# Attention and mixer kernel: row-wise weight loads, strided weight columns, one load on another queue, features one stage earlier

## The chip, the cores and the metric

The kernel runs on one core of one Trainium2 chip. The metric is the device time of one execution in microseconds (us). The five engines are TensorE (PE; its weight loads are listed apart as PEld), VectorE (DVE), ScalarE (ACT), GpSimd (POOL) and SyncE (SP). ACT, POOL and SP also have queues from which DMAs are issued (written ACTq, POOLq, SPq).

## The reference

Linear attention with cosine and sine features, whose output is the input of a token mixer and a channel mixer. There are 8 batches of 8 heads, 576 positions and a head size of 64, all in float32.

```python
q_p = phi(q, cos_w, sin_w)          # relu(x) * cos, relu(x) * sin, side by side: 128 features
k_p = phi(k, cos_w, sin_w)
kv = np.einsum('bhsf,bhsd->bhfd', k_p, v)
z = np.sum(k_p, axis=2)
num = np.einsum('bhsf,bhfd->bhsd', q_p, kv)
den = np.einsum('bhsf,bhf->bhs', q_p, z)[..., None] + 1e-06
x = num / den                       # per batch 576 x 512
h = np.maximum(x.T @ w_tok1, 0.0) @ w_tok2      # 576 -> 256 -> 576, over positions
u = x + h.T
h2 = np.maximum(u @ w_ch1, 0.0) @ w_ch2         # 512 -> 1536 -> 512, over channels
out = u + h2
```

## The kernel before, in words

A batch's 576 positions are four chunks of 128 (row p of the tile holds positions 4p to 4p+3, one to each chunk) and a tail of 64. The tails of two batches share the 128 partitions of one tail tile, so a tail's channel mixer is done once for two batches, in the odd one. Chunks are numbered 0 to 3, the tail is R = 4.

A batch goes through two halves. *Front* (class Front): features of keys (k_side, KS) and queries (q_side, QS), each two DVE instructions (L263) that write kp or qp; values cast to bf16 (values, V: L274 on ACT, L276 elsewhere); kv_ps, the product of features and values (kv, L320); kv_out; the transposes of the query features, by DMA from SP (q_trans_dma, L350), in batches 0 and 1 on PE (q_trans, L340); numerators and division (num, L359 to L369, into x_sb); the token mixer (tok1, tok2: b_ps L382, u_ps L406, u_sb and u_tail L409); the cast of u to bf16 and its transposes by DMA (u_trans_dma L438, tail_trans_dma L443). *Channel* (class Channel): twelve steps c_main(mi), each four matmuls of 128 w_ch1 columns (the stationary operand) with uT into c_ps (L535), and ACT's relu into h1T (L539); in odd batches c_tail does the same for the tail pair with 128 moving columns (ct_ps, L555); then o_step, two matmuls of w_ch2 at a time into o_ps (L568), the addition o_sb on DVE (L573), and the output DMA from SP (L575). Batch 0's first three c_ps are done block by block (L545).

Order on every engine is the order of the program, written out by hand. While Channel of batch b is issued step by step, pieces of Front of batch b+1 are put between the steps. The method pieces lists them as (step, what, arguments): steps 0 to 11 (C + at) are the c steps, from O = 12 on the o steps. Batch 1 has a plan of its own (first), which also holds batch 0's last tok2; batch 2 takes its values some steps later than the others (late). Entries at step -1 are issued just ahead of the channel half. The main loop (L728 to L752) builds the plan at the start of each channel half.

Loads: q, k and v of a batch come as one DMA of 1 MB each and one or two of 128 KB for the tails, all from SP's queue after the start. load_batch(2, "v") stands at step NCH + 13 of batch 0, so on SP it follows the three transposes of batch 1's u (L438 twice, L443). The weights w_ch1 and w_ch2 come from POOL's queue with a cast from float32 to bf16: w_ch1 in four DMAs (two blocks of 128 rows and half the columns each, L184 to L191), w_ch2 in three (four blocks of 128 rows each, L194 to L198). The first w_ch1 load waits for the keys of batch 0, batch 1's loads wait for the second w_ch1 load, and batch 2's keys for the second w_ch2 load.

The hidden channels are in blocks of 128, mi or ki from 0 to 11: c_main writes block mi of h1T, o_step multiplies block ki of h1T by w_ch2[:, ki, :]. The tiles kp and qp have four buffers, PSUM has four of tag mm (c_ps, ct_ps, o_ps and others) and two of tag at.

Of the kernel before, what the change touches and what calls it, by code (L numbers as in the profile page):

```python
# [16 lines left out]
def kernel(  # L17
# [15 lines left out]
    nc = tc.nc  # L33
# [147 lines left out]
        nc.gpsimd.memset(t[half(1)], 0.0)  # L181
    for g in range(2):
        nc.gpsimd.dma_start(out=w_tail1[half(g), :], in_=moe_w_tok1[SM:S, :])
    C2 = D_ch // 2  # L184
    w_ch1_done = []
    for c2 in range(2):
        for ki in range(0, NCC, 2):
            w_ch1_done.append(nc.gpsimd.dma_start(
                out=w_ch1[:, ki:ki + 2, c2 * C2:(c2 + 1) * C2],
                in_=moe_w_ch1[ki * P:(ki + 2) * P, c2 * C2:(c2 + 1) * C2]  # L190
                .rearrange("(n c) d -> c n d", c=P)))  # L191
    after(w_ch1_done[0], k_done)
    w_ch2_done = []
    def load_w_ch2():  # L194
        for ki in range(0, NCH, 4):
            w_ch2_done.append(nc.gpsimd.dma_start(
                out=w_ch2[:, ki:ki + 4, :],
                in_=moe_w_ch2[ki * P:(ki + 4) * P, :].rearrange("(n t) d -> t n d", t=P)))  # L198

# [14 lines left out]
    class Front:  # L216
# [244 lines left out]
        def pieces(self, b, before):  # L461


            first, odd = b == 1, b % 2 == 1
            V, KV, N = self.values, self.kv, self.num
            KS, QS, QT, T = self.k_side, self.q_side, self.q_trans, self.tok2
            C, O = 0, NCH
            if first:

                u, act, pool = before.tok2, nc.scalar, nc.gpsimd  # L470
                plan = [(4, KS, 0), (4, KS, 1), (5, u, 0, ps_at, False), (5, KS, 2, True),
                        (6, KS, 3, True), (6, u, 1, ps_at, False), (7, KS, R), (8, V, 0, act),
                        (8, V, 2, pool), (8, V, 3, pool), (8, load_w_ch2),
                        (8, u, 2, None, False), (9, V, 1, act), (9, u, 3, None, False),
                        (10, u, R, None, False), (10, V, R, nc.vector)]
                plan += [(11, KV, ci) for ci in range(NSC)]
                plan += [(11, QS, 0), (11, QS, 1), (11, self.kv_out),
                         (11, QT, 0, (0, H), act, ps_at), (11, QT, 1), (11, QS, 2), (11, QS, R),
                         (O, QT, 2), (O, N, 0), (O, QS, 3), (O + 1, QT, R, (0, H), act, ps_at),
                         (O + 1, N, 1), (O + 3, N, 2), (O + 3, QT, 3),  # L480
                         (O + 5, N, R), (O + 7, N, 3), (O + 8, before.tail_cast)]
            else:

                late = b == 2
                plan = [(C + at, V, ci, nc.scalar)
                        for ci, at in enumerate((3, 3, 4, 4, 5) if late else (-1, -1, 0, 1, 2))]
                plan += [(C + at, KS, ci) for ci, at in enumerate((0, 0, 1, 2, 2))
                         if ci < R or not odd]
                for ci, at in zip(ORDER, (0, 0, 1, 0, 2) if odd else (1, 2, 3, 4, 5)):
                    if ci < R or not odd:  # L490
                        plan += [(C + at, QS, ci), (C + at, self.q_trans_dma, ci)]

                plan += [(C + at, KV, ci) for ci, at in
                         enumerate((4, 5, 5, 6, 7) if late else
                                   (2, 3, 4, 5, 6) if odd else (2, 3, 4, 6, 7))]
                plan.append((C + (6 if odd else 7), self.kv_out))
            if first:
                at, mix, t = (), O + 7, O + 11
            elif odd:
                at, mix, t = (C + 8, C + 9, C + 10, C + 11, O + 2), O + 3, O + 7  # L500
            else:
                at, mix, t = (C + 9, C + 10, C + 11, O + 1, O + 3), O + 4, O + 8
            plan += [(i, N, ci) for i, ci in zip(at, ORDER)]
            plan += [(mix, self.mix_head, 0), (mix + 1, self.mix_head, 1),
                     (mix + 2, self.mix_tail)]

            plan += [(t + at, T, ci) for ci, at in enumerate((0, 1, 2, 3, 3) if not first else
                                                             (0, 0, 1, 2, 2))]
            plan += [(t + 3 - first, self.u_trans_dma, 3, R)]
            plan.append((t + 2 - first, self.u_trans_dma, 0, 3))  # L510
            if odd:
                plan.append((t + 3 - first, self.tail_trans_dma))
            slots = {}
            for slot, what, *args in sorted(plan, key=lambda p: p[0]):
                slots.setdefault(slot, []).append((what, args))
            return slots
# [4 lines left out]
    class Channel:  # L521
# [7 lines left out]
        def c_main(self, mi, lo=0, hi=SM):  # L529
            if lo == 0:  # L530
                self.c_ps[mi] = ps_mm.tile([P, SM], F32, name="c_ps", tag="mm")
            c_ps = self.c_ps[mi]
            uT = self.res["uT"].rearrange("p (r k) t -> p r k t", r=R)
            for ki in range(NCC):
                nc.tensor.matmul(c_ps[:, lo:hi], w_ch1[:, ki, mi * P:(mi + 1) * P],  # L535
                                 uT[:, lo // P:hi // P, ki, :],
                                 start=(ki == 0), stop=(ki == NCC - 1))
            if hi == SM:
                nc.scalar.activation(self.h1T[:, mi, :], c_ps, AF.Relu)  # L539

        def c_block(self, mi, ki):
            if ki == 0:
                self.c_ps[mi] = ps_mm.tile([P, SM], F32, name="c_ps", tag="mm")
            uT = self.res["uT"].rearrange("p (r k) t -> p r k t", r=R)
            nc.tensor.matmul(self.c_ps[mi], w_ch1[:, ki, mi * P:(mi + 1) * P], uT[:, :, ki, :],  # L545
                             start=(ki == 0), stop=(ki == NCC - 1))
            if ki == NCC - 1:
                nc.scalar.activation(self.h1T[:, mi, :], self.c_ps[mi], AF.Relu)

        def c_tail(self, mi):  # L550

            if mi % R == 0:
                self.ct_ps = ps_mm.tile([P, R, P], F32, name="ct_ps", tag="mm")
            for ki in range(NCC):
                nc.tensor.matmul(self.ct_ps[:, mi % R, :], w_ch1[:, ki, mi * P:(mi + 1) * P],  # L555
                                 self.tail.uT[:, ki, :], start=(mi % R == 0 and ki == 0),
                                 stop=(mi % R == R - 1 and ki == NCC - 1), skip_group_check=True)
            if mi % R == R - 1:
                nc.scalar.activation(self.h1T_tail[:, mi - R + 1:mi + 1, :], self.ct_ps, AF.Relu)
# [140 lines left out]
                c.c_block(mi, kb)  # L700
        return c

    def load_batch(b, which="kvq", behind=None):
        if b not in io_tiles:
            io_tiles[b] = tiles()
        if b // 2 not in io_tails:
            io_tails[b // 2] = tail_tiles()
        qt, vt, kt = io_tiles[b]
        qtt, vtt, ktt = io_tails[b // 2]
        done = []  # L710
        for n in which:
            dst, tail_dst, src = {"k": (kt, ktt, k), "v": (vt, vtt, v), "q": (qt, qtt, q)}[n]
            done.append(load_main(dst, src, b))
            if behind is not None and len(done) == 1:
                after(done[0], behind)
            if b % 2 == 0:
                load_tail(tail_dst, src, b)
            if b % 2 == 0 or b == 1:
                load_tail(tail_dst, src, b | 1)
        return done  # L720


    results = [dict() for _ in range(B)]
    load_batch(1, "kvq", behind=w_ch1_done[1])
    tails = {0: tail0}
    f = Front(0, results[0], tail0)
    c = first_front(f)
    for b in range(B):  # L728
        slots = {}
        if b + 1 < B:  # L730
            if (b + 1) // 2 not in tails:
                tails[(b + 1) // 2] = Tail((b + 1) // 2)
            slots = Front(b + 1, results[b + 1], tails[(b + 1) // 2]).pieces(b + 1, f)
        if b > 0:
            c = Channel(b, results[b], tails[b // 2])
        for what, args in slots.pop(-1, ()):
            what(*args)
        for i, step in enumerate(c.steps(AHEAD if b == 0 else 0)):
            step()
            for what, args in slots.pop(i, ()):  # L740
                what(*args)
# [2 lines left out]
            if b == 0 and i == NCH:  # L744
                load_batch(2, "kq", behind=w_ch2_done[1])
            if b == 0 and i == NCH + 13:
                load_batch(2, "v")
            if 0 < b < B - 2 and i == NSC:
                load_batch(b + 2, "vq")
            if b < B - 3 and i == NCH + (18 if b == 0 else 12):  # L750
                load_batch(b + 3, "k")
        assert not slots  # L752

    _ = tile, bass_utils

# [29 lines left out]
```

## Time and profile before

| what | value |
|---|---|
| median of three runs | 273.86 us (273.8 to 275.31) |
| profiled execution, own time | 273.98 us |
| its span, first to last instruction | 271.8 us |
| granted TensorE clock | 0.997 |
| DVE busy | 165.0 us (61%) |
| ACT busy | 129.7 us (48%) |
| 512-column matmuls of L535 | x360 |
| 128-column matmuls of L555 | x192, 219 ns each |
| weight loads over w_ch1, L535 / L555 | x384 / x192, 97 and 98 ns each |
| w_ch loads, issue to landing | 5.8 / 9.9 / 12.1 us (min, median, max) |

The profile was taken of one execution; its own time lies above its span by what surrounds the first and last instruction. Matmuls are pipelined: a matmul's listed duration runs from its start to the end of its last column, and the next starts before that, so throughput is read from starts, and an idle time in brackets is shorter than what was lost by the starts.

### The profile page before, as it was taken

What the parts mean: (1) busy time and instruction counts of PE and PEld (TensorE: products, weight loads), DVE (VectorE), ACT (ScalarE), POOL (GpSimd) and SP (SyncE); (2) the same over time, 40 slices, a digit from 0 to 9 for tenths busy, and PEclk for the clock granted to TensorE, in tenths of its full rate; (3) what the DMA queues carried; (4) which work ended last, traced back from release to release, by engine and by line L of the source; (5) the groups of instructions that cost most, each with busy time, mean ns of one, the idle gap of its engine ahead of it and who ended that gap; (6) DMA issues with size and microseconds to landing.
All of it is one profiled execution on the core that took longest, in us unless ns stands there. A gap on an engine that the chain in (4) does not pass through costs nothing.

```text
span 271.8 us, 5106 instructions
## 1 busy us (share of the span) xinstructions
PE 260.4 (96%) x2030; PEld 138.6 (51%) x2050; DVE 165.0 (61%) x376; ACT 129.7 (48%) x228; POOL 10.9 (4%) x24
## 2 busy tenths in 40 slices
PE   6989999997999999999999999999999999999994
PEld 2665465454644445446644445446644445445543
DVE  5974888767366477659466567659465567720022
ACT  4955975427616273347606363437606362426400
POOL 6400220000000000000000000000000000000000
PEclk9999999999999999999999999999999999999998
DMA  7999999979994989759994879389974380180032
GB/s 219 344 270 284 326 152 247 309 180 351 189 337 116 268 155 253 229 138 251 160 362 115 277 188 316 111 164 267 217 266 116 116 147 10 41 211 3 2 102 91
DMA packets 91815, 53.68 MB, mean 197 GB/s; under 512 B 59408, under 2 KB 86928, under 8 KB 91792
## 3 DMA queue, kind: packets, MB, share of 16 engines
q1 hardware_dynamic: 88432, 49.62, 67.3%
q0 software_dynamic: 2832, 3.21, 7.2%
q10 hardware_dynamic: 528, 0.52, 0.6%
q8 instruction: 16, 0.26, 0.4%
q14 instruction: 7, 0.06, 0.1%
HBM read 35.85 MB, written 9.44 MB: 167 GB/s over the span
## 4 chain that ended last, share of the span: by engine, by line
PE 77%; DVE 15%; DMA 4%; issue 2%; SPq 1%; ACT 0%; DVEq 0%
PE o_ps L568 32%; PE c_ps L535 19%; PE u_ps L406 6%; PE b_ps L382 6%; DVE qp L263 5%; PE ct_ps L555 4%; DVE kp L263 4%; PE num_ps L359 3%; DVE x_sb L369 3%; PE kv_ps L320 2%; DMA vt<-in_v_dram 2%; DMA qt<-in_q_dram 2%; PE idle_ps L204 1%; PE c_ps L545 1%; DVE den L367 1%
## 5 line engine op out<-in xcount | busy, mean ns | idle before, releaser
L568 PE MATMUL o_ps<-w_ch,h1T 128*128 128x512 bf16 (+1 forms) x381 | 92.5, 372 | 0.5
L535 PE MATMUL c_ps<-uT,w_ch 128*128 128x512 bf16 (+2 forms) x384 | 92.2, 372 | 0.1
L539 ACT ACTIVATE h1T<-c_ps 128x512 bf16<-128x512 f32 x93 | 55.4, 598 | 61.8 <-PE c_ps L535 61.5
L568 PEld LDWEIGHTS <-h1T 128*128 128x128 bf16 x396 | 37.4, 98 | 39.8
L535 PEld LDWEIGHTS <-w_ch 128*128 128x128 bf16 x384 | 33.4, 97 | 29.6 <-issue 0.2
L573 DVE TENSOR_TENSOR o_sb<-o_ps,u_sb 128x512 f32<-128x512 f32 (+1 forms) x33 | 22.3, 675 | 39.8 <-PE o_ps L568 37.2
L409 DVE TENSOR_TENSOR u_sb<-u_ps,x_sb 128x512 f32<-128x512 f32 x32 | 21.9, 690 | 6.3 <-PE u_ps L406 6.2
L413 ACT CAST u_bf<-u_sb 128x512 bf16<-128x512 f32 x28 | 17.3, 618 | 16.9 <-DVE u_sb L409 15.3
L406 PE MATMUL u_ps<-B,w_tok 128*128 128x512 bf16 x79 | 22.4, 379 | 0.2
L387 ACT ACTIVATE B<-b_ps 128x512 bf16<-128x512 f32 x8 | 4.8, 597 | 32.6 <-PE b_ps L382 32.5
L369 DVE TENSOR_TENSOR x_sb<-num_ps,den 128x512 bf16<-128x512 f32 x28 | 19.4, 692 | 1.0
L555 PEld LDWEIGHTS <-w_ch 128*128 128x128 bf16 x192 | 14.0, 98 | 9.2
L382 PE MATMUL b_ps<-x_sb,w_tok 128*128 128x512 bf16 x63 | 17.7, 379 | 0.1
L274 ACT CAST v_aug<-vt 128x512 bf16<-128x512 f32 (+1 forms) x30 | 16.7, 586 | 1.6 <-DMA vt<-in_v_dram 1.6
L263 DVE TENSOR_SCALAR kp<-kt,cos_t 128x512 bf16<-128x512 f32 x32 | 15.2, 480 | 3.7 <-DMA kt<-in_k_dram 3.7
L555 PE MATMUL ct_ps<-uT_tail,w_ch 128*128 128x128 bf16 x192 | 17.2, 219 | 0.0
L263 DVE TENSOR_SCALAR qp<-qt,cos_t 128x512 bf16<-128x512 f32 (+1 forms) x35 | 15.9, 454 | 0.7 <-DMA qt<-in_q_dram 0.7
L263 DVE TENSOR_SCALAR qp<-qt,sin_t 128x512 bf16<-128x512 f32 (+1 forms) x35 | 15.9, 454 | 0.0
L359 PEld LDWEIGHTS <-qpT 128*128 128x128 bf16 x256 | 11.5, 98 | 5.9 <-issue 1.1
L320 PE MATMUL kv_ps<-v_aug,kp 128*128 128x65 bf16 x256 | 12.1, 193 | 2.5 <-ACT v_aug L274 1.6
L573 DVE TENSOR_TENSOR o_sb<-o_ps,u_tail 128x512 f32<-128x512 f32 x4 | 2.8, 692 | 19.2 <-PE o_ps L568 19.2
L359 PE MATMUL num_ps<-kv_sb,qpT 128*128 128x65 bf16 x256 | 13.0, 193 | 1.3 <-DVE x_sb L369 1.0
(93 smaller groups left out, 219.3 us busy)
## 6 DMA issues: line engine op xcount, KB each, us to landing
out_dram<-o_sb SPq DMA_DIRECT2D x31, 256.0 KB, 3.1
kt<-in_k_dram SPq DMA_DIRECT2D x7, 1024.0 KB, 6.9
vt<-in_v_dram SPq DMA_DIRECT2D x7, 1024.0 KB, 6.4
qt<-in_q_dram SPq DMA_DIRECT2D x7, 1024.0 KB, 8.4
w_ch<-in_moe_w_ch_dram POOLq DMA_DIRECT2D x4, 384.0 KB, 10.5
w_ch<-in_moe_w_ch_dram POOLq DMA_DIRECT2D x3, 512.0 KB, 8.5
out_dram<-o_sb SPq DMA_DIRECT2D x10, 128.0 KB, 2.3
qtt<-in_q_dram SPq DMA_DIRECT2D x8, 128.0 KB, 6.6
```

The costliest lines, as they stand in the source:

```text
L263: nc.vector.tensor_scalar(o_ap, i_ap, scalar1=w, scalar2=0.0, op0=ALU.mult, op1=ALU.max)
L320: nc.tensor.matmul(self.kv_ps[g][:, j * DP:j * DP + D1], self.k_of(ci)[:, g * HH + j, :, :] .rearrange("p a b -> p (a b)"), self.va[:, ci, ...
L359: nc.tensor.matmul(num_ps[:, g, j * DP:j * DP + D1], self.qT_of(ci, h), self.kv_sb[g][:, j, 0:D1], start=True, stop=True)
L369: nc.vector.tensor_mul(self.x_of(ci)[rows].rearrange("p (g j d) -> p g j d", g=2, j=HH), nv[:, :, :, 0:D], den.to_broadcast([rows.stop - r ...
L382: nc.tensor.matmul(self.b1_ps[mi], w, self.x_of(ci), start=(ci == ORDER[0]), stop=(ci == ORDER[-1]))
L406: nc.tensor.matmul(u_ps, w_tok2[:, ki, ci * P:(ci + 1) * P], self.B1[:, ki, :], start=(ki == 0), stop=(ki == NT - 1))
L409: nc.vector.tensor_add(u, u_ps[rows], self.x_of(ci)[rows])
L535: nc.tensor.matmul(c_ps[:, lo:hi], w_ch1[:, ki, mi * P:(mi + 1) * P], uT[:, lo // P:hi // P, ki, :], start=(ki == 0), stop=(ki == NCC - 1))
L539: nc.scalar.activation(self.h1T[:, mi, :], c_ps, AF.Relu)
L555: nc.tensor.matmul(self.ct_ps[:, mi % R, :], w_ch1[:, ki, mi * P:(mi + 1) * P], self.tail.uT[:, ki, :], start=(mi % R == 0 and ki == 0), s ...
L568: nc.tensor.matmul(o_ps, h, w_ch2[:, ki, cols], start=ki == 0, stop=ki == NCH - 1)
L573: nc.vector.tensor_add(o_sb, o_ps, u)
```

## The change

- w_ch1 is loaded in four DMAs of 128 whole rows each. w_ch2 is loaded with four neighbouring rows to a partition (t n) instead of four rows that lie 128 apart (n t), so each partition's part is one run in DRAM.
- So that the hidden channels stand in the same order on both sides, block mi of w_ch1 takes every fourth column of a group of 512: w_ch1_of(ki, mi) is a view with a step of four elements, and all matmuls over w_ch1 use it as stationary operand.
- Batch 2's values (three DMAs) are issued from ACT's queue instead of SP's, at the same place of the program.
- Batch 1: its tail values (V, R on DVE) move from step 10 to 7, its first query side from 11 to 9.
- Batches 2 to 7: the order of key and query sides is written anew. Two sides go to four and three steps before the end of the channel half before (for even batches key chunks 0 and 1, for odd ones key chunk 0 and query chunk 0 with its transpose), and the plan of the next batch is built there.

```diff
-    C2 = D_ch // 2
-    w_ch1_done = []
-    for c2 in range(2):
-        for ki in range(0, NCC, 2):
-            w_ch1_done.append(nc.gpsimd.dma_start(
-                out=w_ch1[:, ki:ki + 2, c2 * C2:(c2 + 1) * C2],
-                in_=moe_w_ch1[ki * P:(ki + 2) * P, c2 * C2:(c2 + 1) * C2]
-                .rearrange("(n c) d -> c n d", c=P)))
+    NR = 4
+    w_ch1_done = [nc.gpsimd.dma_start(out=w_ch1[:, ki, :], in_=moe_w_ch1[ki * P:(ki + 1) * P, :])
+                  for ki in range(NCC)]
+    def w_ch1_of(ki, mi):
+        z, n = divmod(mi, NR)
+        return w_ch1[:, ki, z * NR * P:(z + 1) * NR * P].rearrange("c (t n) -> c n t", n=NR)[:, n, :]
...
-                in_=moe_w_ch2[ki * P:(ki + 4) * P, :].rearrange("(n t) d -> t n d", t=P)))
+                in_=moe_w_ch2[ki * P:(ki + NR) * P, :].rearrange("(t n) d -> t n d", t=P)))
...
-                        (6, KS, 3, True), (6, u, 1, ps_at, False), (7, KS, R), (8, V, 0, act),
+                        (6, KS, 3, True), (6, u, 1, ps_at, False), (7, KS, R), (7, V, R, nc.vector), (8, V, 0, act),
                         (8, V, 2, pool), (8, V, 3, pool), (8, load_w_ch2),
                         (8, u, 2, None, False), (9, V, 1, act), (9, u, 3, None, False),
-                        (10, u, R, None, False), (10, V, R, nc.vector)]
+                        (9, QS, 0), (10, u, R, None, False)]
...
-                plan += [(C + at, KS, ci) for ci, at in enumerate((0, 0, 1, 2, 2))
-                         if ci < R or not odd]
-                for ci, at in zip(ORDER, (0, 0, 1, 0, 2) if odd else (1, 2, 3, 4, 5)):
-                    if ci < R or not odd:
-                        plan += [(C + at, QS, ci), (C + at, self.q_trans_dma, ci)]
+                if odd:
+                    sides = ((-4, KS, 0), (-3, QS, 0), (0, KS, 1), (0, KS, 2), (1, QS, 1),
+                             (1, KS, 3), (1, QS, 2), (2, QS, 3))
+                else:
+                    sides = ((-4, KS, 0), (-3, KS, 1), (0, KS, 2), (1, KS, 3), (1, QS, 0),
+                             (2, KS, R), (2, QS, 1), (3, QS, 2), (4, QS, R), (5, QS, 3))
+                for at, side, ci in sides:
+                    plan.append((C + at, side, ci))
+                    if side == QS:
+                        plan.append((C + at, self.q_trans_dma, ci))
...
-                nc.tensor.matmul(c_ps[:, lo:hi], w_ch1[:, ki, mi * P:(mi + 1) * P],
+                nc.tensor.matmul(c_ps[:, lo:hi], w_ch1_of(ki, mi),
...
             if b == 0 and i == NCH + 13:
-                load_batch(2, "v")
+                load_batch(2, "v", eng=nc.scalar)
...
+            if i == len(steps) - 4 and b + 2 < B:
+                following = next_front(b + 2)
+            for what, args in following.pop(i - len(steps), ()):
+                what(*args)
```

## The prediction

> **What bounds the kernel now.** I read the page first (span, busy shares), then PE's waits, then the chain of waits around the longest of them, then the timeline around the others. The page:
>
> ```profile
> span 271.8 us, 5106 instructions
> PE 260.4 (96%) x2030; PEld 138.6 (51%) x2050; DVE 165.0 (61%) x376; ACT 129.7 (48%) x228; POOL 10.9 (4%) x24
> ```
>
> TensorE is busy in 96% of the span, at a granted clock of 0.997. So only what lets PE start a matmul sooner, or makes its stream slower, changes the time. PE's own waits (us in total, times, longest):
>
> ```profile
> PE kv_ps L320 <- ACT v_aug L274: 1.6, 1, 1.6
> PE qT_ps L340 <- DVE qp L263: 1.2, 3, 0.7
> PE kv_ps L320 <- DVE kp L263: 0.9, 3, 0.3
> ```
>
> These three are what the change can reach. The longest is in the channel stage of batch 1; the chain of waits shows what made the values late:
>
> ```profile
> 54.48 0.62 ACT ub_tail L416
> 55.10 1.18 SPq L438
> ...
> 56.38 1.22 SPq L443
> 57.59 0.05 issue
> 57.65 6.21 DMA vt<-in_v_dram
> 63.86 0.02 issue
> 63.88 0.63 ACT v_aug L274
> 64.51 0.04 issue
> 64.55 0.40 PE kv_ps L320 x8
> ```
>
> The load of batch 2's values stands on SP's queue behind three transposes, of which the last two wait for ACT's casts; it goes out at 57.65, lands 6.21 later, and PE waits. The third wait comes three times, once in the stage that prepares each of batches 3, 5 and 7 (98.80, 159.63, 220.47). The timeline of the first (start, duration, instruction):
>
> ```profile
> 92.51 0.69 DVE L573 TENSOR_TENSOR o_sb<-o_ps,u_sb 128x512 f32<-128x512 f32 x1 [1.90 <-PE o_ps L568]
> 97.47 1.03 PE L535 MATMUL c_ps<-uT,w_ch 128*128 128x512 bf16 x4
> 98.26 0.48 DVE L263 TENSOR_SCALAR kp<-kt,sin_t 128x512 bf16<-128x512 f32 x1
> 98.80 0.42 PE L320 MATMUL kv_ps<-v_aug,kp 128*128 128x65 bf16 x8 [0.30 <-DVE kp L263]
> ```
>
> DVE starts the features only after the batch's last o_sb (92.51); the fourth chunk's are ready at 98.74. Four c_ps matmuls pass in 0.86 (the chain's c_ps x4 pieces), so PE was free at 97.47 + 0.86 = 98.33 and lost 0.47. The second chunk before it came 0.10 late in the same way (97.21, after matmuls from 96.25).
>
> **The change part by part.** The sum is made against this execution's own 273.98 us (span 271.8 and about 2.1 around it); the median of the three runs is 273.86, so I carry the same number over less 0.1.
>
> *Values of batch 2 on ACT's queue.* ACT reaches the issue when ub_tail's cast ends, 54.48 + 0.62 = 55.10, which is 2.55 before SP did. Three DMAs cost ACT about 0.5 + 2 x 0.65 = 1.8 (the rows of the same two loads on the queues); ACT has idled 4.91 before its row at 60.01, so this is covered. With the same 6.21 the data lands at 61.3; it now shares the DMA engines with the two last transposes (512 KB landing until 58.8), for which I add up to 0.7: 62.0. ACT's four activations end at 60.01 + 2.31 = 62.32, so ACT itself is late next: the cast ends at 62.95, and kv_ps starts at 63.0 instead of 64.55. Gain 1.55. SP loses three issues, so the k load and the query transposes behind them go out earlier; the first of those transposes now waits for the landing of the values too (their semaphore is reused), at 62.0 still before the 63.92 of now.
>
> *Features moved forward.* Two sides (four instructions, 1.6 us at 0.40 apart) move to four and three steps before the end of the stage before, into DVE's idle 1.90 in front of its last o_sb; the cover is thin (0.3), and past it o_sb frees one of four PSUM buffers late. After that o_sb (ends 93.2), kp of chunks 1 and 2 are ready at 94.8, and of chunk 3 at 96.4, with kv_ps asking at 97.1 and 98.2. Both losses go: 3 x (0.47 + 0.10) = 1.7. For even batches no wait of PE stands there, so I count nothing. Of the moved query sides the SP transpose goes along, ahead of the last output: 1.27 of SP time (a row of 1.27 for one), and no one waits for that output.
>
> *Batch 1.* Its tail values move ahead of two u_sb additions on DVE, and the first query side ahead of u_tail; these now queue behind the two loads (vtt issued 24.09 and at most 8.3 to landing, qt 26.76 and at most 8.8), which are there at 32.4 and 35.6, before DVE comes to them. qp of chunk 0 comes at about 36.3 instead of 38.1, of chunk 1 at 37.8 instead of 38.9, but kv_sb still holds DVE until about 39.0, so chunk 2 comes only some 0.2 to 0.3 sooner, and the numerators pass on that. Gain 0.3; the bounds are 0 and the 0.8 of the two later rows.
>
> *Loads of w_ch.* Bytes stay; the runs in DRAM get longer (w_ch1 from 3 KB to 6 KB, w_ch2 from 2 KB to 8 KB). The fourth w_ch1 load, issued at 13.1, took at most the group's 12.1 and lands by 25.2. Whole rows make PE need it at its tenth first matmul, 24.33 + 9 x 0.216 = 26.3, where so far half the columns would do. 1.1 spare: cost nothing, gain nothing; if longer runs save time, o_ps at 39.47 has its w_ch2 sooner.
>
> *Columns of w_ch1 in steps of four.* 588 weight loads (384 of L535, 192 of L555, 12 of L545) now read elements 8 bytes apart. No load of the trace is strided, so I bound it. Contiguous loads follow each other very closely, and PE's shortest stream over w_ch1 is L555:
>
> ```profile
> 12.19 0.27 PEld L285 LDWEIGHTS <-kp 128*128 128x128 bf16 x8 [0.32 <-DVE kp L263]
> 73.64 0.83 PE L555 MATMUL ct_ps<-uT_tail,w_ch 128*128 128x128 bf16 x12
> ```
>
> Eight loads of 96 ns end within 270, so (270 - 96)/7 = 25 ns from one to the next; the twelve matmuls of 219 take (830 - 219)/11 = 55.5 each. A load may thus get 2.2 times slower before L555 feels it, and 8 times before the 512-column matmuls do (216 ns). The only strided read in the trace is ACT's, four f32 apart, against its contiguous twin:
>
> ```profile
> L210 ACT CAST w_tok<-u_sb 128x512 bf16<-128x512 f32 x2 | 2.2, 1112 | 2.0 <-DMA u_sb<-in_moe_w_tok_dram 2.0
> L207 ACT CAST w_tok<-u_sb 128x512 bf16<-128x512 f32 x2 | 1.2, 619 | 0.0
> ```
>
> 1.8 times slower at 16 bytes' step. As a load that is 45 ns, still hidden: cost 0, and nothing excludes the other end, where a strided load doesn't overlap the next at all and takes its whole 98 ns (L555's row): (192 + 12 with 128 columns in L535) x (98 - 55.5) = 8.7. I take 0, the nearest row being ACT's. The Trainium skill, "SBUF — State Buffer", Specifications, says that full bandwidth needs two hits on a 16-byte line: ACT's 16-byte step has one hit and is slower, the new 8-byte step has two, so by that rule the loads do not slow at all, and the sum is the same. Against the change speaks "TensorE: Matmul & The Clock Gate", Weight-path perf modes, of the Trainium skill: the fast load reads 32 bits at a time, two bf16, which a step of four splits; by it a load would take twice as long, some 50 ns (an estimate), which is also under 55.5. No row here shows either.
>
> Sum: 273.98 - 1.55 - 1.7 - 0.3 = 270.4.
>
> **The rivals.** *Slower: strided loads bind L555.* If a load takes more than 55.5 ns in a row, 204 matmuls pay the rest. It decides at 3.55/204 = 17 ns more, an interval of 73 ns; at 98 the time is 270.4 + 8.7 = 279.1. For it: the loads have no strided twin in the trace. Against: ACT's factor of 1.8. The Trainium skill, "TensorE: Matmul & The Clock Gate", LDWEIGHTS (loading the stationary operand), gives a load as its columns divided by 1.2, 107 ns; with no overlap the cost by that would be 10.5 (an estimate from that page) and the time 281.
>
> *The values don't come sooner, or something else does not.* If the load and the transposes share so badly that one of them is late, uT_tail (asked for at 60.19) waits or the cast does; the 1.55 is lost or paid elsewhere: 272.0, up to 272.6. For it: DMA is busy 0.91 to 0.95 of these stages. Against: the transposes' 512 KB are little beside 1 MB. The Trainium skill, "DMA: Bandwidth & Descriptors", Issuing engines are not separate DMA queues, says that another issuer saves only sequencer time; here that time is the 2.55 that SP spends waiting, so by that rule the gain stands.
>
> *Features forward bring nothing,* since o_sb comes late or the numerators then wait: 1.7 lost, 272.1. Against: numerators begin at 101.88 and their transposes go out sooner too.
>
> *It does not do what it says:* both gains gone, 273.6.
>
> **How the numbers follow.** About 1% (2.7 us) is what a measurement of this kernel can tell from no change. Forecast 0.56, its own range 269.4 to 271.4; strided loads 0.20 (from 273 to 281, some of it within 1%); values 0.12; features 0.07; nothing 0.05. Faster than 271.1 comes from most of the forecast: 0.50. Slower than 276.6: 0.16 of the first rival. The rest, 0.34, is within 1%. For 8 in 10 the range runs from 269.4 over the second to fourth rival into the first, as far as 276.5.
>
> **What would show it.** Right: the v load issued by ACT near 55 and kv_ps near 63.0; no wait of kv_ps for kp in the stages of batches 3, 5 and 7; twelve L555 matmuls still in 0.83; PE's busy time unchanged. Wrong: L555's twelve taking over 1 us, an o_sb after features that PE waits for, c_ps waiting for uT_tail, or u_ps and qT_ps waits in batch 1 that did not shrink.

## The result, and the profile after

The changed kernel takes 275.34 us (median of 20 runs, 273.79 to 278.16); the kernel before, on the same chip, 273.99 us (20 runs). The ratio is 1.0042, 95% interval 1.0028 to 1.0056: 0.4% slower, where 1.3% faster was predicted.

The page of the profiled execution after the change:

```profile
span 275.4 us, 5105 instructions
PE 263.2 (96%) x2030; PEld 146.5 (53%) x2050; DVE 164.7 (60%) x376; ACT 129.5 (47%) x228; POOL 13.2 (5%) x24
PEclk9999999986999999999999999999999999999999
```

This execution took 277.42 us, 2.1 more than the median, and its granted clock is 0.988, where most runs of the kernel show 0.998 to 1.0; so its details are not all typical, and the sizes below rest on timed experiments. PE's waits after (us in total, times, longest):

```profile
PE c_ps L542 <- DMA uT<-u_bf: 4.0, 1, 4.0
PE idle_ps L205 <- POOL ident masks.py:199: 1.4, 1, 1.4
PE num_ps L360 <- DVE x_sb L370: 1.0, 2, 0.5
```

The three waits that the prediction showed (kv_ps for v_aug and for kp, qT_ps for qp) are gone from this list; a longer one has come: the first c_ps of batch 1 waits 4.0 us for u's DMA transposes, uT. Three timelines show how (PE; SP's queue; ACT's queue: start, duration, instruction):

```profile
53.33 4.48 PE L575 MATMUL o_ps<-w_ch,h1T 128*128 128x512 bf16 x20
61.76 5.31 PE L542 MATMUL c_ps<-uT,w_ch 128*128 128x384 bf16 x24 [3.96 <-DMA uT<-u_bf]
```

```profile
53.64 3.02 SPq L439 DMA_TRANSPOSE uT<-u_bf  x2
56.75 1.34 SPq L444 DMA_TRANSPOSE uT_tail<-ub_tail  x1
```

```profile
54.61 0.37 ACTq L86 DMA_DIRECT2D vt<-in_v_dram  x1
55.18 1.77 ACTq L92 DMA_DIRECT2D vtt<-in_v_dram  x2
```

The transposes go out when they did (53.6), and c_ps, which started at 57.57 before, starts at 61.76. The view of the tile uT has the time from issue to landing, before and after:

```profile
DMA to landing us min/median/max: 2.4/2.9/3.4
```

```profile
DMA to landing us min/median/max: 8.1/8.3/8.5
```

The values' load went out at 54.61 on the other queue, just behind the first of them; whether it made them late is tested below. The wait has a sequel in this execution, seen in the stretches by time (columns: stretch, length, busy time of PE, PEld, DVE, ACT and POOL with instructions, granted clock, DMA share, GB/s):

```profile
54.00:58.00 4.00, 3.81 (x18) 1.55 (x16) 2.94 (x7) 1.06 (x2) 0.00 (x0) 1.00 1.01 118
58.00:62.00 4.00, 0.24 (x1) 0.15 (x2) 4.00 (x10) 0.00 (x0) 0.00 (x0) 0.80 1.07 258
62.00:66.00 4.00, 4.00 (x16) 2.09 (x15) 2.87 (x8) 0.00 (x0) 0.00 (x0) 0.50 1.17 327
```

The clock falls while PE is still idle (0.80 is the mean of the second stretch), and in the third, which the row calls fully busy, PE has time for 16 matmuls at a clock of 0.50.

### The profile page after: what moved, and what is told of

It is laid out like the page before. It is cut to its first block, busy times and chain, and to the rows that moved or that the text cites. A ratio compares the mean times of both kernels' runs of the same rounds, so it can differ in the third digit from the quotient of the medians.

```text
span 275.4 us, 5105 instructions
## 1 busy us (share of the span) xinstructions
PE 263.2 (96%) x2030; PEld 146.5 (53%) x2050; DVE 164.7 (60%) x376; ACT 129.5 (47%) x228; POOL 13.2 (5%) x24
## 4 chain that ended last, share of the span: by engine, by line
PE 76%; DMA 14%; DVE 4%; POOL 2%; SPq 1%; issue 1%; POOLq 0%
PE o_ps L575 31%; PE c_ps L542 25%; PE u_ps L407 6%; PE b_ps L383 5%; DMA w_ch<-in_moe_w_ch_dram 4%; DMA vt<-in_v_dram 4%; PE ct_ps L562 4%; DMA uT<-u_bf 3%; PE kv_ps L321 3%; DMA kt<-in_k_dram 3%; DVE x_sb L370 3%; PE num_ps L360 2%; POOL w_ch L186 2%; DVE den L368 1%; DVE den L369 1%
## 5 line engine op out<-in xcount | busy, mean ns | idle before, releaser
L542 PE MATMUL c_ps<-uT,w_ch 128*128 128x512 bf16 (+2 forms) x384 | 95.0, 382 | 4.0 <-DMA uT<-u_bf 4.0
L542 PEld LDWEIGHTS <-w_ch 128*128 128x128 bf16 x384 | 39.4, 116 | 31.3 <-DMA uT<-u_bf 4.4
L562 PEld LDWEIGHTS <-w_ch 128*128 128x128 bf16 x192 | 15.5, 114 | 8.0
L562 PE MATMUL ct_ps<-uT_tail,w_ch 128*128 128x128 bf16 x192 | 17.4, 220 | 0.0
L332 DVE CAST kv_sb<-kv_ps 128x260 bf16<-128x260 f32 x8 | 3.5, 433 | 23.2 <-ACT kv_sb L332 23.2
```

Of the source, the lines that this page charges most:

```text
L542: nc.tensor.matmul(c_ps[:, lo:hi], w_ch1_of(ki, mi), uT[:, lo // P:hi // P, ki, :], start=(ki == 0), stop=(ki == NCC - 1))
L562: nc.tensor.matmul(self.ct_ps[:, mi % R, :], w_ch1_of(ki, mi), self.tail.uT[:, ki, :], start=(mi % R == 0 and ki == 0), stop=(mi % R == R ...
```

## The experiments

Theory M: the values' load on a second queue makes the transposes of batch 1's u late. Rivals: W, the loads and strided reads of w_ch do it; F, the features moved forward do it. All ratios are to the kernel before, timed beside each kernel, with 95% intervals.

**The parts, one by one.** The changed kernel with the values back on SP's queue:

```
-                load_batch(2, "v", eng=nc.scalar)
+                load_batch(2, "v")
```

> The changed kernel, with only batch 2's values back on SP's queue. Theory (the values' load on a second queue runs beside the transposes of batch 1's u and makes them late): the two uT transposes land about 2.5 to 3.5 us after issue again (8.1 and 8.5 us in the changed kernel), PE's wait of 4.0 us for uT before the first c_ps of batch 1 goes, the granted clock stays at 1.0 behind it, and the wait of kv_ps for v_aug (1.6 us before) comes back. The kp waits stay away. Time 271.9 to 272.6 us, below both kernels. Rival W (the loads of w_ch1 and w_ch2, or the strided weight loads, make uT late): the wait stays, 275 us. Rival F (the features moved forward delay u): the wait stays, 275 us.

273.11 us, 0.9966 (0.995 to 0.9982): below before, but 0.5 us above what was expected. The wait for uT is gone, v_aug's is back (1.3 us), and there is a wait not foreseen, t_ps for B, 1.2 us.

The kernel before with only the values on ACT's queue (the same lines, added to it):

> The kernel before, with only batch 2's values on ACT's queue. Theory: the new wait of about 4 us for uT appears here too, the v_aug wait of 1.6 us goes, so about 276.5 us, and up to 279 us where the granted clock drops behind the wait. By the step of the prediction (values sooner, transposes hardly touched) 272.4 to 273.1 us. Rivals W and F: no wait for uT, 272.4 us.

276.11 us, 1.0079 (1.0054 to 1.0103). Its first wait, and the landing of uT:

```profile
PE c_ps L535 <- DMA uT<-u_bf: 3.2, 2, 1.9
```

```profile
DMA to landing us min/median/max: 5.4/6.7/8.0
```

The part alone makes the wait: 3.2 us against the 1.6 us that it removes. M holds.

The kernel before with only the features moved forward (the edits of the plans, slots and main loop):

> The kernel before, with only the features moved forward (batch 1's plan and the sides of batches 2 to 7). Theory: the waits of kv_ps for kp in batches 3, 5 and 7 go (3 x 0.57 us), a new wait of 0.43 us for u_sb in batch 1 at about 36 us comes: 272.2 to 272.8 us. Rival F: a wait for uT of some us appears and the time is 275 us or more. Rival that features bring nothing: 274.0 us.

271.61 us, 0.9916 (0.9896 to 0.9936). PE's waits have no kp left; one of 0.3 us for w_ch2 has come in, since o_ps of batch 0 now starts earlier. F falls: this part is worth 2.3 us, 0.6 us more than the upper end of what was expected, and the foreseen wait for u_sb did not come.

The kernel before with only the layout of w_ch1 and w_ch2 and the strided columns:

> The kernel before, with only the new layout of w_ch1 and w_ch2 and the columns of w_ch1 read in steps of four. Theory: weight loads over w_ch1 take 115 ns instead of 98 ns but stay hidden behind the matmul that runs, and what is left is 0 to 0.3 us: 273.9 to 274.4 us. Rival W: 275 us or more, with idle time of PE at c_ps or ct_ps.

275.52 us, 1.0054 (1.0037 to 1.0072): expected at 0, it costs 1.5 us, yet no c_ps or ct_ps waits. The chain of waits in batch 0 shows where:

```profile
10.37 10.57 DMA u_sb<-in_moe_w_tok_dram
20.94 0.02 issue
20.96 1.10 ACT w_tok L210
22.07 0.20 ACT w_tok L212
22.27 1.00 ACT w_tok L210
23.27 0.20 ACT w_tok L212
23.47 0.50 ACT B L387
23.97 0.05 issue
24.02 1.90 PE t_ps L433 x8
```

The load of w_tok2 (it lands in a tile named u_sb) takes 10.57 us beside w_ch1, ACT permutes it, and ACT's relu B stands behind that. The first c_ps of batch 0 starts at 25.75 instead of 24.25, and these 1.5 us stay to the end of the trace. In the kernel before it landed 2 us sooner and was just in time, as ACT's timeline there shows:

```profile
19.00 1.12 ACT L210 CAST w_tok<-u_sb 128x512 bf16<-128x512 f32 x1 [1.99 <-DMA u_sb<-in_moe_w_tok_dram]
21.62 0.60 ACT L387 ACTIVATE B<-b_ps 128x512 bf16<-128x512 f32 x1
```

The last of the permutes ended at 21.53, B's input came at about 21.6: some 0.1 us to spare.

The parts add up: -0.84% + 0.79% + 0.54% = +0.49%, measured +0.42% (0.28 to 0.56).

**Rows or stride?** Only w_ch1's loads by whole rows, columns read side by side:

```
-    for c2 in range(2):
-        for ki in range(0, NCC, 2):
...
+    w_ch1_done = [nc.gpsimd.dma_start(out=w_ch1[:, ki, :], in_=moe_w_ch1[ki * P:(ki + 1) * P, :])
+                  for ki in range(NCC)]
```

> The kernel before, with w_ch1 loaded by whole rows and nothing else (its columns are read side by side as before). The new layout alone gave +1.5 us, and its trace has a wait of 1.1 us of t_ps for B in batch 0: w_tok2 landed at 20.94 instead of 18.97 us while w_ch1 was on its way. Theory L (w_ch1's loads by whole rows take bandwidth from the load of w_tok2): w_tok2 lands at 20 us or later, t_ps waits about 1 us, time 275.0 to 275.6 us. Rival S (the strided weight loads cost the time): no such wait, 273.9 us.

275.47 us, 1.0053 (1.0041 to 1.0065), t_ps waits 0.7 us for B, w_tok2 lands at 20.50. Only the rest (w_ch2's rows, strided columns, w_ch1 loaded as before):

> The kernel before, with the new rows of w_ch2 and the columns of w_ch1 in steps of four, but w_ch1 loaded as before. Theory L: w_tok2 lands near 19 us, t_ps does not wait, weight loads of L535 and L555 take 115 ns, time 273.7 to 274.3 us. Rival S: 275.0 to 275.6 us.

274.36 us, 1.0020 (1.0005 to 1.0035). Here w_tok2 landed at 20.18 in the profiled execution, and t_ps waited 0.4 us, though w_ch1's loads are those of before: when w_tok2 lands varies between executions too. Over all traces in which nothing holds w_ch1, it took 10.5 to 10.6 us in three with the new rows, and 8.5 to 8.9 us in nine with the old ones, with 10.2 in this one as the exception; in two (the changed kernel and the one with several steps, below) it took 6.5 to 6.8 us. So the rows cost most, and that they slow w_tok2 is likely, but not free of exceptions. Of the 0.9 us that this trace is longer than that of before, 0.8 are lost when the first c_ps starts, so the strided columns and w_ch2's rows can have cost it 0.15 us at most.

How a weight load's duration and PE's pace go with the step:

```
+                if mi < 3:
+                    nc.tensor.matmul(c_ps[:, lo:hi], w_ch1[:, ki, 0:P], mv, **flags)
+                elif mi < 6:
+                    nc.tensor.matmul(c_ps[:, lo:hi], w_ch1[:, ki, 0:2 * P:2], mv, **flags)
+                elif mi < 9:
+                    nc.tensor.matmul(c_ps[:, lo:hi], w_ch1[:, ki, 0:4 * P:4], mv, **flags)
+                else:
+                    nc.tensor.matmul(c_ps[:, lo:hi], w_ch1[:, ki, 0:12 * P:12], mv, **flags)
```

> The kernel before, with the stationary operand of the matmuls over w_ch1 read at other places: columns side by side for hidden blocks 0 to 2, in steps of two elements for 3 to 5, of four for 6 to 8, of twelve for 9 to 11, each on a line of its own. The channel mixer's weights are then other columns than the reference's; loads, counts and shapes are the same. Theory: the weight load's duration rises with the step (98 ns side by side, 114 ns at four), and at twelve is between 115 and 200 ns; the pace of the 128-column matmuls of ct_ps (55.5 ns from start to start) stays, so the time is that of before within 0.3 us. Rival 1 of the prediction (the load binds): starts of ct_ps are further apart at steps of four or twelve, time over 274.5 us.

Weight loads by line (L537 side by side, L539 steps of two, L541 of four, L543 of twelve; the second number behind the bar is the mean in ns):

```profile
L543 PEld LDWEIGHTS <-w_ch 128*128 128x128 bf16 x96 | 12.0, 147 | 4.2
L541 PEld LDWEIGHTS <-w_ch 128*128 128x128 bf16 x96 | 9.5, 114 | 6.2
L537 PEld LDWEIGHTS <-w_ch 128*128 128x128 bf16 x96 | 9.0, 98 | 9.5
L539 PEld LDWEIGHTS <-w_ch 128*128 128x128 bf16 x96 | 8.1, 98 | 6.6 <-issue 0.2
```

98, 98, 114 and 147 ns. From start to start, ct_ps over steps of one, two and four are equally close (55.9 ns), over steps of twelve 5 ns further apart, and those of c_ps 8 ns. The time, 274.85 us (1.0031, 1.0020 to 1.0041), is above what was expected; steps of twelve explain about 0.8 us of it (72 intervals of c_ps by 8.0 ns and 44 of ct_ps by 4.7 ns above those side by side, from the starts), and o_ps waited 0.6 us for w_ch2. Four is hidden, twelve no longer quite.

**Queue, moment or bytes?** Half of the values' main load on ACT's queue (kernel before):

```
+            if b == 2 and n == "v":
+                load_main(dst, src, b, 0, HH, nc.scalar)
+                done.append(load_main(dst, src, b, HH, H))
```

> The kernel before, with half of batch 2's values (heads 0 to 3, 512 KB) on ACT's queue and the other half and the tails on SP's as before. Theory M: the delay of the transposes goes with the bytes that run beside them: the wait for uT is 0.8 to 2.5 us (3.2 us for the whole 1.28 MB on ACT's queue), partly paid back by the v_aug wait of 1.6 us, which shrinks or goes; 274.0 to 275.5 us. Rival Q2 (a second queue with anything in it costs the whole delay): a wait of 3 us or more, 276 us. By the step of the prediction: below 273.9 us.

274.38 us, 1.0021 (1.0003 to 1.0039), a wait for uT of 0.7 us: 0.5 MB cost 0.7 us, 1.28 MB cost 3.2. M holds, Q2 falls. The whole load on ACT's queue, but issued when the transposes have landed:

```
-            if b == 0 and i == NCH + 13:
+            if b == 1 and i == 0:
                 load_batch(2, "v", eng=nc.scalar)
```

> The kernel before, with batch 2's values on ACT's queue, but issued one step into batch 1, behind ACT's relu of its first c_ps, that is when the transposes of u have landed. Theory M (what hurts is the time at which the load starts, beside the transposes, not the queue as such): uT lands 2.4 to 3.4 us after issue, no wait for uT, the values land about 1 to 2 us later than before, and kv_ps waits 1.6 to 3.5 us for v_aug: 274.0 to 276.0 us. Rival Q (any load on a second queue slows what SP's queue holds): qpT or kt land later by some us and new waits appear behind 70 us, or uT still waits.

280.63 us, 1.0252 (1.0235 to 1.0269). uT lands by 57.50, as before, so it is not the queue as such; but the cost is far above the expected. Batch 3's keys, now ahead on SP, go first, the values land at 69.3, and PE's timeline has

```profile
60.75 1.02 PE L535 MATMUL c_ps<-uT,w_ch 128*128 128x512 bf16 x4
64.22 1.02 PE L535 MATMUL c_ps<-uT,w_ch 128*128 128x512 bf16 x4 [2.22 <-ACT h1T L539]
70.01 0.60 PE L320 MATMUL kv_ps<-v_aug,kp 128*128 128x65 bf16 x8 [4.43 <-ACT v_aug L274]
70.42 1.90 PE L535 MATMUL c_ps<-uT,w_ch 128*128 128x512 bf16 x4
```

The first wait is ACT's: issuing the two tail loads held it for 2.92 us, with relus behind. Behind the second wait (4.43 us) four matmuls take 1.90 us instead of 1.02. But the clock had fallen before that wait began, some 1 us after the first one ended (columns as above):

```profile
61.80:65.20 3.40, 1.18 (x11) 0.58 (x9) 3.40 (x9) 1.57 (x3) 0.00 (x0) 1.00 1.02 328
65.20:65.60 0.40, 0.38 (x5) 0.22 (x3) 0.40 (x2) 0.00 (x0) 0.00 (x0) 0.52 0.93 282
65.60:70.00 4.40, 0.00 (x0) 0.00 (x0) 0.88 (x3) 0.66 (x2) 0.00 (x0) 0.50 1.21 292
```

**Is w_tok2 what the layout costs?** The changed kernel, values on SP, w_ch1 held until w_tok2 has landed; then the same hold in the old layout with the features; then the latter with batch 2's kv_ps later as well:

```
-    after(w_ch1_done[0], k_done)
+    after(w_ch1_done[0], tok2_done)
```

> The changed kernel with batch 2's values on SP's queue and the first w_ch1 load waiting for w_tok2's landing instead of for the keys'. Theory L: w_tok2 lands near 16 us instead of 20.8 us, t_ps no longer waits for B (1.2 us with the values on SP's queue alone), w_ch1 still lands ahead of its matmuls: 271.5 to 272.2 us, against 273.1 us without the wait. Rival: w_ch1 now comes late and PE waits for it or for what is loaded behind it (batch 1's keys, w_ch2), 273 us or more.

> The kernel before with the features moved forward and the first w_ch1 load waiting for w_tok2's landing (w_ch1 and w_ch2 as before). Theory L: with the old layout w_tok2 was in time by itself, so nothing is won over the 271.6 us of the features alone: 271.4 to 271.9 us; what the kernel with the new layout and the same wait has above this is the price of the strided weight loads and the new rows, 0 to 0.4 us. Rival: below 271.2 us, if the old layout too lost time at w_tok2; above 272 us, if w_ch1 or what follows comes late.

> The kernel before with the features moved forward, w_ch1 behind w_tok2, and batch 2's kv_ps matmuls one or two channel steps later (steps 6, 6, 7, 7, 8 instead of 4, 5, 5, 6, 7, kv_out at 8), so that the channel steps run while the values are on their way: values still from SP's queue. Theory (the 1.3 us wait for v_aug is an order of the program, and the channel steps can fill it): the wait goes, no wait for kv_sb at the first numerator comes: 270.0 to 270.7 us. Rival: num_ps waits for kv_sb, or the numerators come late for the token mixer, and 0.7 us or more is given back: 271 us or more.

275.03 us (1.0038, 1.0017 to 1.0058), 275.85 (1.0058, 1.0037 to 1.0080) and 275.84 (1.0057, 1.0038 to 1.0076). All three miss; the rival of the first two has it, and the third carries the same hold: w_tok2 lands at 16.49 in the first, but w_ch1 goes out at 16.77 instead of 10.5, with 4.5 us to its first landing, and the loads behind it (batch 1's, w_ch2) land 2.9 to 4.0 us later than with the values on SP alone. In the first kernel PE then waits for w_ch1:

```profile
26.15 0.84 PE L552 MATMUL c_ps<-uT,w_ch 128*128 128x512 bf16 x3 [0.40 <-DMA w_ch<-in_moe_w_ch_dram]
28.12 0.84 PE L552 MATMUL c_ps<-uT,w_ch 128*128 128x512 bf16 x3 [1.13 <-DMA w_ch<-in_moe_w_ch_dram]
```

In the other two DVE waits 8.1 and 7.5 us for batch 1's keys, and PE 2.3 us for DVE's u_sb. In the second kernel the clock fell behind this wait, though it was that short; in the third, with a wait of the same length, it did not:

```profile
37.50:40.90 3.40, 1.22 (x6) 0.58 (x6) 3.18 (x5) 1.61 (x4) 3.33 (x5) 1.00 0.42 79
41.00:44.30 3.30, 3.30 (x52) 3.30 (x51) 2.32 (x7) 1.02 (x3) 0.00 (x0) 0.50 1.06 165
```

A shorter hold, until batch 0's last values have landed:

```
-    after(w_ch1_done[0], k_done)
+    after(w_ch1_done[0], v_done)
```

> The changed kernel with batch 2's values on SP's queue (273.1 us) and the first w_ch1 load waiting for the last values of batch 0, which land near 14.0 us, instead of for its keys (10.3 us). Theory L: w_tok2 lands at 16 to 18 us, t_ps does not wait, w_ch1 lands within 1 us of where it did, and the time is 271.6 to 272.3 us. Rival B (each hold of w_ch1 shifts the loads behind it): w_ch1 and batch 1's loads land 1 to 3 us later and PE waits for them near 25 to 45 us: 273 us or more.

272.29 us, 0.9924 (0.9896 to 0.9953), without it 0.9966: w_tok2 lands at 16.94, t_ps no longer waits, and the time is within 0.1% of the features alone. The intervals just touch, so the size is likely rather than settled.

**What is the values' wait worth?** All of these have the features forward in the old layout. First, batch 2's kv_ps one or two steps later; to that, the shorter hold alone; instead of the hold, ACT's casts one step later; to the last, batch 3's keys behind batch 2's qpT transposes:

```
-                         enumerate((4, 5, 5, 6, 7) if late else
+                         enumerate((6, 6, 7, 7, 8) if late else
...
-                plan.append((C + (6 if odd else 7), self.kv_out))
+                plan.append((C + (8 if late else 6 if odd else 7), self.kv_out))
...
-                        for ci, at in enumerate((3, 3, 4, 4, 5) if late else (-1, -1, 0, 1, 2))]
+                        for ci, at in enumerate((4, 4, 5, 5, 6) if late else (-1, -1, 0, 1, 2))]
...
+            if b == 1 and i == NSC:
+                load_batch(3, "k")
...
-            if b < B - 3 and i == NCH + (18 if b == 0 else 12):
+            if 0 < b < B - 3 and i == NCH + 12:
```

> The kernel before with the features moved forward (271.6 us) and batch 2's kv_ps matmuls one or two channel steps later (steps 6, 6, 7, 7, 8 and kv_out at 8), all loads as in the kernel before. Theory: the 1.3 us wait of kv_ps for v_aug goes and nothing comes in its place: 270.0 to 270.7 us. Rival: the numerators wait for kv_sb and give it back: 271.2 us or more.

272.04 us, 0.9912 (0.9885 to 0.9939): nothing won over 0.9916. PE's waits say why:

```profile
PE ct_ps L562 <- ACT h1T L546: 0.9, 1, 0.9
PE c_ps L542 <- ACT h1T L546: 0.7, 1, 0.7
```

ACT's cast waits for the values as before, the relus stand behind it, and PE runs out of c_ps buffers.

> As the run before (features forward, kv_ps later), and w_ch1 held until the last values of batch 0 have landed. Theory L: in the old layout w_tok2 is in time without that, so nothing is won or lost: within 0.4 us of the run before. Rival B: 1 us or more above it.

272.87 us, 0.9956 (0.9933 to 0.9980): here the hold cost some 0.4% (the two intervals just touch), o_ps waiting 1.0 us for w_ch2. In the old layout it has nothing to mend.

> As the run with kv_ps later (272.0 us; 0.9912 of before), and batch 2's casts of the values one step later too (steps 4, 4, 5, 5, 6 instead of 3, 3, 4, 4, 5), so that ACT does not stand at a cast while the relu of step 4 is ready. Theory: the waits of ct_ps and c_ps for h1T near 65 us go: 270.4 to 271.0 us, a ratio of 0.985 to 0.988 to before. Rival: the casts that come later hold up kv_ps or kv_sb, and the ratio stays at 0.990 or above.

272.00 us, 0.9920 (0.9905 to 0.9935). The waits for h1T are gone; in their place:

```profile
PE num_ps L360 <- DMA qpT<-qp: 1.4, 1, 1.4
```

> As the last run (features forward, casts and kv_ps of batch 2's values later; 0.992 of before), and batch 3's keys loaded behind batch 2's last qpT transpose instead of ahead of its first. Theory (the stretch is bound by bytes in transit): qpT lands 2 to 4 us sooner, num_ps no longer waits for it, 270.2 to 270.9 us, a ratio of 0.985 to 0.988. Rival (the transposes are late by themselves): num_ps still waits 1 us or more, 0.991 or above.

271.07 us, 0.9876 (0.9856 to 0.9895): num_ps no longer waits for qpT. Its first transpose lands at 67.56 instead of 71.06: it goes out 2.1 us sooner, since SP has neither the keys to issue nor an output behind them that took 2.52 us to issue, and it takes 6.0 us to land instead of 7.4. SP's queue before and after, and PE's short list:

```profile
63.65 6.72 SPq L351 DMA_TRANSPOSE qpT<-qp  x3
```

```profile
61.55 6.25 SPq L351 DMA_TRANSPOSE qpT<-qp  x3
```

```profile
PE idle_ps L205 <- POOL ident masks.py:199: 1.4, 1, 1.4
PE num_ps L360 <- DVE x_sb L370: 1.0, 2, 0.5
PE o_ps L575 <- DMA w_ch<-in_moe_w_ch_dram: 0.9, 1, 0.9
```

It is the fastest kernel of this study, 1.2% below before. The keys alone, casts and kv_ps at their old steps:

> The kernel before with the features moved forward (0.9916 of before), and batch 3's keys loaded later in the same way, with casts and kv_ps at their old steps. Theory: the values share with less and land 0.5 to 1.5 us sooner than 63.4 us, so the v_aug wait of 1.3 us shrinks by as much: 270.1 to 271.1 us, a ratio of 0.985 to 0.990. Rival: the values land at the same time, 0.991 to 0.993; or the keys of batch 3 come late for its features, above 0.993.

272.34 us, 0.9940 (0.9918 to 0.9963): the values land 6.5 us after issue, no sooner than before, and v_aug's wait stays (1.5 us); c_ps waits 0.7 us for uT and o_ps 0.6 us for qpT besides. So far as one run tells, the step back of the keys pays only once the consumers have moved.

## Why the prediction was wrong, step by step

*Values of batch 2 on ACT's queue:* predicted -1.55, alone +2.2 us. This step failed, at "it now shares the DMA engines with the two last transposes ... for which I add up to 0.7". ACT issued it at 54.6 (foretold: 55.1), and v_aug's wait went. But the step asked what the transposes cost the values, not what the values cost the transposes. The transposes' packets waited behind the values' (in the trace's packet records of that part alone, none of the transposes' between 57 and 59 us), and uT landed 5.4 and 8.0 us after issue. Rival 2 named this mechanism for uT_tail, asked for at 60.19, and capped it at 272.6. In the kernel before, uT_tail landed at 58.78, 1.4 us ahead; the one with the least slack was uT's first transpose: the first c_ps needs only its three chunks (384 columns), they landed at 56.93, and c_ps began at 57.57, 0.64 us later. In the part alone they landed at 59.03; 1.3 us were lost there, and 1.9 more at the fourth chunk. "512 KB are little beside 1 MB" argued for the wrong side: the little one is what waits. (512 KB is the size of uT's two transposes together; the last two hold half of that.) The Trainium skill, "DMA: Bandwidth & Descriptors", Issuing engines are not separate DMA queues, says that all queues run on the same 16 engines and interleave, and that another issuer saves only sequencer time. That they share, the runs confirm; but the second issuer did more than save 2.55 us of SP: it changed the order of service, and the interleaving was far from even (2.9 to 6.7 us in the median for the transposes).

*Features moved forward, and batch 1:* predicted -1.7 and -0.3, together -2.0; alone -2.3 us (1.8 to 2.8 by the interval). Right, mechanism and size: between the traces of before and of this part alone, the stages that prepare batches 3, 5 and 7 are 0.6 us shorter each (1.8 in all) and batch 1's is 0.3 shorter; another 0.3, from a shorter wait for v_aug, was not forecast. The timeline after has no idle ahead of batch 3's kv_ps:

```profile
97.39 2.75 PE L542 MATMUL c_ps<-uT,w_ch 128*128 128x512 bf16 x12
99.98 0.19 PE L321 MATMUL kv_ps<-v_aug,kp 128*128 128x65 bf16 x1
```

*Loads of w_ch:* predicted "cost nothing, gain nothing", alone 1.5 us for the layout, 1.4 of it the rows. This step failed too, since it followed w_ch1's own landing (it came in time, as said) and no other load in transit at that moment. The row that would have shown it stands in the prediction for another purpose: L210, 2.0 us idle "<-DMA u_sb", ACT waiting for w_tok2 with 0.1 us to spare behind it. Whether a typical execution of the changed kernel loses this time too is inferred from the parts: in its profiled execution w_tok2 landed early, at 16.21. There the first w_ch1 issue held POOL for 4.49 us (0.56 in the trace of the layout alone), and the other three went out some 3 us later.

*Columns in steps of four:* predicted 0. Rival 1 (279.1) is refuted. The loads take 116 and 114 ns instead of 97 and 98, and L555's twelve matmuls, now L562, still take 0.83:

```profile
L542 PEld LDWEIGHTS <-w_ch 128*128 128x128 bf16 x384 | 39.4, 116 | 31.3 <-DMA uT<-u_bf 4.4 <-issue 2.0
L562 PEld LDWEIGHTS <-w_ch 128*128 128x128 bf16 x192 | 15.5, 114 | 8.0
```

```profile
78.72 0.83 PE L562 MATMUL ct_ps<-uT_tail,w_ch 128*128 128x128 bf16 x12
```

ACT's factor of 1.8 was no measure of a weight load; it is 1.17 at this step. The two rules that the prediction set beside it, no slowing at 8 bytes and a load twice as long, did not come out either. PE's pace did not change, so the cost of 0 was right as far as the runs tell.

*The sum.* With measured terms it is -2.3 + 2.2 + 1.5 = +1.4 us on 273.99, 275.4; measured 275.34. Each part has an interval of some 0.5 us either way, so that it comes this close is partly luck. The forecast's -3.6 was wrong by two terms, and what they share is that both were priced by the moved load and not by what was in transit beside it.

*The 1.55 itself* did not come by a load on ACT's queue, whole, half or late; an earlier place on SP's own queue was not tried. With the wait taken from PE's product it came back behind ACT's casts, then at the numerators; only when 1 MB of keys went behind the transposes as well did the time fall (0.9920 to 0.9876). Whether that is won by fewer bytes beside the transposes (6.0 us to land instead of 7.4) or by their earlier place on SP's queue (2.1 us) is not told apart; the values themselves landed no sooner (6.4 us after issue, 6.1 in the run before).

## What to carry to other kernels

Before a load is moved to another queue, list every transfer in transit between its new issue and its landing, and for each the time from landing to first use; the price is set by the one with the least slack, here 0.6 us for uT and 0.1 us for w_tok2, and not by the load itself. A queue that makes a load stand behind others is also what protects those others. If a wait moves on when it is removed (product, casts, numerators), look at what else the queues carry in that stretch before moving more instructions.

## What the runs showed of the hardware

- Idle PE and its clock: in the clock records of all 20 traces the granted clock changes only on a grid of 3.41 us, from step to step. At the end of 23 steps it fell from 1.00 to 0.50, three times within a kernel (the waits of 3.96, 2.22 and 2.31 us above) and 20 times behind the last matmuls. In each of these steps PE was idle for 2.02 us or more; in all other steps at 1.00, some 1,500, for 1.95 us or less. So a wait of 2.31 us cost half the clock for 3.41 us in one kernel, and one of 2.30 us, parted between two steps, nothing in another. The Trainium skill, "TensorE: Matmul & The Clock Gate", Part 1: The HAM clock gate (the "warmup" mystery), has the clock halve after at least one idle window of about 3.4 us; the length agrees with the steps seen here, but a step need not be idle throughout. From some 2 us on, a late transfer can thus cost more than its own wait.
- A weight load of 128 columns in bf16 takes 98 ns at steps of one and two elements, 114 at four, 147 at twelve; PE's pace at 128 moving columns feels it only at twelve, by 5 ns.
- DMA issues on ACT are not always short: two 128 KB loads held ACT for 2.92 us in the late load's kernel, against 1.77 in the changed kernel.
- Holding w_ch1 until another load had landed cost its round trip: 4.5 to 5.1 us from issue to its first landing, and in the first of these kernels the loads behind it landed 2.9 to 4.0 us later.
